# Parallel attention and gated-GELU block: which engine adds the second P-times-V bank, and in which slots a unit's scores and masks stand

## The chip, the cores and the metric

The program runs on one core of a Trainium2 chip. The metric is device time in microseconds of one execution. The core has five engines that run their own instruction queues in order: TensorE (PE in the profile; its weight loads are shown as PEld), VectorE (DVE), ScalarE (ACT), GpSimd (POOL) and SyncE (SP, which here only issues DMAs). Matmuls write into PSUM, eight banks of 128 partitions by 512 f32 columns; POOL does not touch PSUM in this kernel.

## The reference, cut to what matters

```python
x = A_x                                        # (1, 2048, 640)
xn = layernorm(x)
q, k, v = split(xn @ wqkv)                     # 32 heads of 20
scores = q @ k.T * 20 ** -0.5
mask = (i - j >= 0) & (i - j < 256)            # sliding window of 256 keys
o = softmax(where(mask, scores, -1e9)) @ v     # "P times V"
h = gelu(xn @ w_gate) * (xn @ w_up)            # 1728 wide
return x + o @ wo + h @ w_down
```

Everything is f32. The kernel reaches that precision by splitting operands into a high and a low part and adding three products.

## The kernel before, in words

**Stages.** A first stage normalises and transposes x. The second, the attention, takes about half of the span. Then come the rest of the gate and up products, and last the down projection and the output projection. The change touches the attention stage alone.

**Units.** The 32 heads are cut into 8 groups of 4, the 2048 queries into 4 chunks of 512, so there are 32 units `u`, with chunk `c = u % 4`. `attention()` (L789) runs 33 rounds of `NS = 14` slots; round `u` computes the scores of unit `u` and, in its slot 0, P times V of unit `u - 1`. The order of PE's, ACT's, DVE's and POOL's instructions in this stage is the order in which the Python code emits them (`manual_schedule`). SP is not in that list: the order of its DMAs is chosen by the framework's planner, so DMAs can be issued earlier than the slot in which the code names them.

**What a slot emits.** First the actions due in it (`tick()`; `defer(n, fn)` sets an action `n` slots later). Then, in some slots, two pairs of row maxima (`pull_max`, `max_pair`, L461): matmuls into two buffers `ps_m` out of a ring of four (`psm`), and two DVE reductions (L490), each followed by a short read of its accumulator. The maxima run ahead of the scores by two units. In slot 0 two pairs come before P times V and two behind. Then scores (`exp_piece`, L531): for score `s` of a unit, `s // 4` is the bank of keys and `s % 4` the head; PE writes `ps_e` (L545), ACT takes the exponential into P (L547). Last, `pull_fill(RATE / NS)` emits 42.2 / 14, about three, matmuls of the projection work that fills the slots (L105). Small DVE operations of that work which fall due are put in a list (`late`) and emitted by `flush()`.

**Two PSUM buffers shared.** Scores and P times V share a ring of two buffers (`psx`, tag "ex"). P times V takes both at once: `os[0]` and `os[1]`, the sums over the lower and the upper 64 key rows of each block. The next unit's score 0 takes the buffer of `os[0]`, score 1 that of `os[1]`; each waits until the buffer has been read out.

**Read-out before.** ACT copies `os[0]` to `ob` (L592) and `os[1]` to `oc`, a part of the old P (L593); three slots later POOL adds the two (`join`, L596); five slots later five DMAs store `ob` (L600, L601).

**Masks.** `pieces(c)` (L512) lists the three banks of P in the order X, Z, Y. One slot after a bank's fourth head, `clear` (L551) lets POOL zero what lies outside the window, four heads in one instruction (L558 for the diagonal, L561 for the far edge): X three instructions, Y three, Z two in chunks 1 to 3; in chunk 0, where P has no earlier keys, two, three and one. Scores stand in the odd slots 1 to 11, two a slot; in slot 1 one fill matmul is emitted between the two. So X is masked in slot 4, Z in slot 8 and Y in slot 12, and P times V (L586) starts two slots after that.

**Loads.** `load_stack` (L446) loads the q and k tiles of unit `u + 3`, six DMAs each (L455); the code names k in slot 9 and q in slot 12. The k buffer being overwritten is that of unit `u - 1`, which unit `u` still reads in X and Z.

Of the kernel before, what the change touches and what calls it, by code (L numbers as in the profile page):

```python
# [19 lines left out]
C = 512  # L20
# [11 lines left out]
RATE = 42.2  # L32
V1_SLOT = 158
MXD = 7
KSLOT = 9
LAG = 3, 5, 4, 4, 4, 4, 3, 3, 4, 3, 2, 1, 1, 1
NFA = 6
HD = D // 2
# [27 lines left out]
def block_kernel(ctx, tc, x, wqk, wv, wgu, wdo, wdl, out):  # L66
    nc = tc.nc
# [130 lines left out]
    def at(slot, fn, *a):  # L198
        acts.setdefault(slot, []).append((fn, a))
# [244 lines left out]
    ap = pr.enter_context(tc.tile_pool(name="ap", bufs=2, side="right", reuse_waits="tile"))  # L444

    def load_stack(u, which=(0, 1)):  # L446
        g, c = divmod(u, NC)
        for m in range(80 * g // 128, (80 * g + 79) // 128 + 1):
            assert all((m + 5 * i, c) in done for i in which), (u, m)

        for i in which:
            dst, src, top, again = ((qs[u % NQ], qd[c], 1, 2), (ks[u % NK], kd[c], 0, 0))[i]
            for j in (0, 2):
                for p, part, n in ((j * 32, top, 2), (j * 32 + 2 * DH, again, 1), (64 - j * 32, 0, 3)):
                    nc.sync.dma_start(dst[p:p + DH * n, j:j + 2].rearrange("p j t -> p (j t)"),  # L455
                                      src[g, part:part + n].rearrange("s (d j) t -> (s d) (j t)",
                                                                      j=4)[:, j * C:(j + 2) * C])
# [54 lines left out]
    def pieces(c):  # L512
        b = 4 * c
        X = [(b, 0, 0, 384)] + ([(b - 2, 384, 0, 128)] if c else [])
        Y = [(b + 1, 0, 128, 384), (b + 3, 384, 384, 128)]
        Z = ([(b - 1, 0, 0, 256)] if c else []) + [(b + 2, 256, 256, 256)]
        return X, Z, Y

    def diag_tail(kb, col, q0, n, c):
        r = []  # L520
# [8 lines left out]
    pts = {}  # L529

    def exp_piece(u, s):  # L531
        g, c = divmod(u, NC)
        bi, j = divmod(s, 4)
        bank = pieces(c)[bi]
        q = qs[u % NQ]
        if j == 0:
            pts[u, bi] = ap.tile([128, 4, C], F32, name="P", tag="P", bufs=3)
        pt = pts[u, bi]
        lo = min(p[1] for p in bank)
        hi = max(p[1] + p[3] for p in bank)  # L540
        ps = psx.tile([128, C], F32, name="ps_e", tag="ex")
        for kb, col, q0, n in sorted(bank, key=lambda p: p[3]):
            k = ks[(u - (kb < 4 * c)) % NK]
            kc = kb % 4 * 128
            nc.tensor.matmul(ps[:, col:col + n], k[0:QROWS, j, kc:kc + 128], q[0:QROWS, j, q0:q0 + n],  # L545
                             start=True, stop=True)
        nc.scalar.activation(pt[:, j, lo:hi], ps[:, lo:hi], AF.Exp, scale=SCALE)  # L547
        if j == 3:
            defer(1, clear, u, bi)

    def clear(u, bi):  # L551
        c = u % NC
        pt = pts[u, bi]
        for p in pieces(c)[bi]:
            for col, diag in diag_tail(*p, c):
                a = pt[:, :, col:col + 128]
                if diag:
                    nc.gpsimd.affine_select(out=a, in_=a, pattern=[[0, 4], [1, 128]], compare_op=OP.is_ge,  # L558
                                            fill=0.0, base=0, channel_multiplier=-1)
                else:  # L560
                    nc.gpsimd.affine_select(out=a, in_=a, pattern=[[0, 4], [-1, 128]], compare_op=OP.is_ge,  # L561
                                            fill=0.0, base=-1, channel_multiplier=1)

    def av_unit(u):
        g, c = divmod(u, NC)
        v = vtiles[g]
        os = [psx.tile([128, C], F32, name="ps_o", tag="ex") for _ in range(2)]
        place = {kb - 4 * c: (pts[u, bi], col, q0) for bi, bank in enumerate(pieces(c)) for kb, col, q0, n in bank}

        def half(d, r):  # L570
            i = 2 * d + r
            return d, r, max(0, 64 * i), min(C, 64 * i + 320)

        steps_ = [((0, 0), (0, 1)), ((2, 0), (-1, 1)), ((-1, 0), (2, 1)), ((1, 0), (1, 1)),
                  ((3, 0), (-2, 1)), ((-2, 0), (3, 1))]
        todo = [half(*x) for pair in steps_ for x in pair if x[0] in place]
        begun_, left = set(), [sum(t[1] == r for t in todo) for r in range(2)]
        for d, r, qa, qb in todo:
            pt, col, q0 = place[d]
            kb = 4 * c + d  # L580
            assert (id(v), kb) in done, (u, kb)
            left[r] -= 1
            rows = slice(64 * r, 64 * r + 64)
            for j in range(4):
                w0_ = kb * 84 + 21 * j
                nc.tensor.matmul(os[r][32 * j:32 * j + 32, qa:qb], v[rows, w0_:w0_ + 32],  # L586
                                 pt[rows, j, col + qa - q0:col + qb - q0], start=r not in begun_,
                                 stop=not left[r], skip_group_check=True, tile_position=(64 * r, 32 * j))
            begun_.add(r)
        ob, oc = ap.tile([128, C], F32, name="ob", tag="ob", bufs=1), pts[u, 2][:, 0]  # L590
        lo = 0 if c else 64
        nc.scalar.activation(ob, os[0], AF.Copy)  # L592
        nc.scalar.activation(oc[:, lo:], os[1][:, lo:], AF.Copy)  # L593

        def join():
            nc.gpsimd.tensor_tensor(out=ob[:, lo:], in0=ob[:, lo:], in1=oc[:, lo:], op=OP.add)  # L596
# [169 lines left out]
    NU = NG * NC  # L766
    stream = ((u, i) for u in range(NU) for i in range(8))
    fill = filler()
    debt = [0.0]

    def pull_max(n, slot):
        for _ in range(n):
            x = next(stream, None)
            if x is None:
                return
            max_pair(*x)
            if x[1] == 7:
                at(slot + (MXD if slot >= 0 else 4), max_end, x[0])

    def tick():  # L780
        todo = [y for t in sorted(t for t in acts if t <= now[0]) for y in acts.pop(t)]
        return sorted(todo, key=lambda y: y[0] is max_end)

    def pull_fill(n):
        debt[0] += n
        while debt[0] > 0:
            debt[0] -= next(fill, 1.0)

    def attention():  # L789
        now[0] = -1  # L790
        load_stack(0)
        load_stack(1)
        load_stack(2)
        for i, (p, k, half) in enumerate((p, k, half) for p in range(NC // 2) for k in range(2) for half in range(2)):
            for j, fn in enumerate(x_sums(p, k, half)):
                at(XS0 + XSN * i + 2 * j, fn)
        for i in range(12):
            now[0] = i - 13
            for fn, a in tick():
                fn(*a)  # L800
            if i % 2 == 0:
                pull_max(2, now[0])
            flush()
            pull_fill(2 * RAMP)
        pull_fill(GAP)
        for u in range(NU + 1):
            for i in range(NS):
                T = now[0] = NS * u + i
                for fn, a in tick():
                    fn(*a)  # L810
                if i in (0, 5, 9) or T == 3:
                    pull_max(2, T)
                if i == 0 and u:
# [599 lines left out]
    for n, (p, k) in enumerate(steps):  # L1413
        i = n % (NQD + 1)
# [71 lines left out]
```

## Time and profile before

| | |
|---|---|
| median of 3 runs | 1060.9 us (1057.14 to 1061.3) |
| the profiled execution's own time | 1059.57 us |
| its span | 1057.7 us |
| granted PE clock | 0.998 |
| PE busy | 1042.1 us (99%) |
| PE weight loads busy | 837.7 us (79%) |
| DVE, ACT, POOL busy | 722.2, 532.1, 376.0 us |
| first and last P times V | 106.1 and 624.9 us from the span's start |

One round of 14 slots takes about 16.8 us, a slot about 1.2 us. In the timeline a row is one or more like instructions that follow each other: its start, its length, engine, line, operation, and in brackets the idle time of that engine before it with what ended it. PE's ends are modelled: a matmul that waits can be shown as busy because the one before it is drawn long, so waits are read both from PE and from PEld rows.

### The profile page before, as it was taken

To read this page: it belongs to the slowest core of one execution; us is meant where nothing else is said; L and a number is where in the kernel's file an instruction comes from. 1 tells how busy PE (TensorE), PEld (TensorE's weight loads), DVE (VectorE), ACT (ScalarE), POOL (GpSimd) and SP (SyncE) were. 2 spreads that over 40 slices of the span, in tenths; PEclk is the share of its full clock that TensorE was granted. 3 is DMA by queue.
4 is the path that set the end of the run, shared out by engine and by line. 5 is a ranking of instruction groups with operands and counts; after the bars stand their busy time and mean duration, and the time that the engine had idled before them with its cause. 6 is when DMAs were issued, how large, how long until landed. Compare 5 with 4: busy or idle time off the path is not lost.

```text
span 1057.7 us, 25616 instructions
## 1 busy us (share of the span) xinstructions
PE 1042.1 (99%) x9429; PEld 837.7 (79%) x9429; DVE 722.2 (68%) x1985; ACT 532.1 (50%) x1120; POOL 376.0 (36%) x550
## 2 busy tenths in 40 slices
PE   8999999999999999999999999999999999999998
PEld 7977666666678766676666778888888999999998
DVE  7745656565554566766666537787775869888887
ACT  4434665566756566565665665223324544333332
POOL 6021765778664484647556451111100000000000
PEclk9999999999999999999999999999999999999999
DMA  5552353546453253434334125576667774443333
GB/s 204 186 157 71 106 175 109 149 122 191 128 159 94 77 167 102 148 100 138 106 111 128 41 82 198 185 252 235 232 234 265 257 235 128 127 138 110 122 128 105
DMA packets 105190, 158.74 MB, mean 150 GB/s; under 512 B 15420, under 2 KB 60092, under 8 KB 105064
## 3 DMA queue, kind: packets, MB, share of 16 engines
q1 hardware_dynamic: 102680, 150.95, 44.7%
q10 hardware_dynamic: 2384, 6.16, 1.8%
q8 instruction: 74, 1.21, 0.5%
q14 instruction: 52, 0.43, 0.1%
HBM read 101.78 MB, written 54.92 MB: 148 GB/s over the span
## 4 chain that ended last, share of the span: by engine, by line
PE 82%; DVE 6%; POOL 4%; issue 3%; DMA 3%; ACT 2%; SPq 1%; ACTq 0%; DVEq 0%; POOLq 0%
PE ps_d L105 24%; PE ps L1202 17%; PE ps_g L935 16%; PE ps_e L545 7%; PE ps_v L105 6%; PE ps_o L586 5%; PE ps_m L480 4%; POOL pt L247 1%; PE ps_g L105 1%; DVE junk L490 1%; DVE ss L1040 1%; POOL P L561 1%; POOL P L558 1%; DMA hr<-hd 1%; DMA stg<-wtd 1%
## 5 line engine op out<-in xcount | busy, mean ns | idle before, releaser
L490 DVE CUSTOM_DVE_ANT_0 junk<-ps_m,mask 128x320 bf16<-128x320 f32 (+2 forms) x512 | 243.1, 475 | 166.2 <-PE ps_m L480 108.4
L547 ACT ACTIVATE P<-ps_e 128x512 f32<-128x512 f32 (+2 forms) x384 | 198.7, 571 | 94.7 <-PE ps_e L545 85.4
L1202 PE MATMUL ps<-wb,at 128*128 128x320 f32 x999 | 157.1, 310 | 2.2 <-DVE at L1040 2.2
L1202 PEld LDWEIGHTS ps<-wb,at 128*128 128x128 f32 x999 | 149.6, 189 | 3.0 <-DVE at L1040 2.7
L105 PE MATMUL ps_d<-xh,wql 128*128 128x512 f32 x430 | 131.4, 415 | 0.0
L105 PE MATMUL ps_d<-xl,wqh 128*128 128x512 f32 x430 | 130.2, 412 | 0.0
L105 PE MATMUL ps_d<-xh,wqh 128*128 128x512 f32 x430 | 130.0, 413 | 0.0
L558 POOL TENSOR_SCALAR_AFFINE_SELECT P<-P 128x512 f32<-128x512 f32 x128 | 83.5, 653 | 102.7 <-ACT P L547 100.3
L545 PE MATMUL ps_e<-qs,ks 124*128 124x128 bf16 (+2 forms) x704 | 117.7, 278 | 0.7 <-ACT P L547 0.4
L105 PEld LDWEIGHTS ps_d<-xl,wqh 128*128 128x128 f32 x430 | 78.7, 189 | 15.0 <-issue 1.6
L105 PEld LDWEIGHTS ps_d<-xh,wql 128*128 128x128 f32 x430 | 78.4, 189 | 14.6 <-issue 1.2
L1202 PE MATMUL ps<-wt,at 128*128 128x320 f32 x552 | 90.0, 312 | 0.0
L105 PEld LDWEIGHTS ps_d<-xh,wqh 128*128 128x128 f32 x430 | 78.2, 189 | 14.6 <-issue 1.1
L545 PEld LDWEIGHTS <-ks 124*128 124x128 bf16 x704 | 49.6, 98 | 50.3 <-issue 36.7
L1202 PEld LDWEIGHTS ps<-wt,at 128*128 128x128 f32 x552 | 83.8, 189 | 0.2
L561 POOL TENSOR_SCALAR_AFFINE_SELECT P<-P 128x512 f32<-128x512 f32 x112 | 71.2, 646 | 27.8 <-ACT P L547 27.8
L1156 ACT ACTIVATE at<-ss 128x512 fp32r<-128x512 f32 x59 | 37.3, 632 | 86.5 <-DVE ss L1040 86.5
L586 PE MATMUL ps_o<-P,v 64*32 64x320 f32 (+4 forms) x2816 | 76.0, 348 | 1.1 <-POOL P L561 0.8
L247 POOL TENSOR_TENSOR pt<-r,pt 128x512 bf16<-128x512 f32 x40 | 46.6, 1166 | 76.8 <-ACT pt L246 75.3
L586 PEld LDWEIGHTS ps_o<-P,v 64*32 64x32 f32 x2816 | 48.5, 106 | 26.8 <-POOL P L561 3.6
L480 PE MATMUL ps_m<-ks,qs 60*64 60x320 bf16 (+3 forms) x1472 | 62.6, 260 | 3.0 <-DVE mx L490 1.2
L480 PEld LDWEIGHTS <-qs 60*64 60x64 bf16 x1472 | 28.2, 105 | 41.9 <-issue 37.2
(195 smaller groups left out, 1742.8 us busy)
## 6 DMA issues: line engine op xcount, KB each, us to landing
hr<-hd SPq DMA_DIRECT2D x104, 128.0 KB
hd<-he SPq DMA_DIRECT2D x50, 256.0 KB
wr<-wgu SPq DMA_DIRECT2D x27, 320.0 KB
qs<-qd SPq DMA_DIRECT2D x64, 120.0 KB
ks<-kd SPq DMA_DIRECT2D x64, 120.0 KB
xi<-x SPq DMA_DIRECT2D x16, 320.0 KB
qs<-qd SPq DMA_DIRECT2D x64, 80.0 KB
ks<-kd SPq DMA_DIRECT2D x64, 80.0 KB
```

Of the source, the lines that this page charges most:

```text
L105: nc.tensor.matmul(ps, a(k), b(k), start=n == 0, stop=n == 3 * nk - 1)
L247: nc.gpsimd.tensor_tensor(out=pt[:, l, :], in0=r, in1=pt[:, 1, :], op=OP.subtract)
L480: nc.tensor.matmul(ps[64 * h:64 * h + 64, col:col + w], q[rows, j, q0:q0 + 64], ks_, start=True, stop=True, tile_position=(64 * r, 64 * h))
L490: nc.vector.tensor_tensor_reduce(out=junk[:, 0:n], in0=ps[:, 320 - n:320], in1=mask[:, 320 - n:320], scale=1.0, scalar=NEG, op0=OP.add, op ...
L545: nc.tensor.matmul(ps[:, col:col + n], k[0:QROWS, j, kc:kc + 128], q[0:QROWS, j, q0:q0 + n], start=True, stop=True)
L547: nc.scalar.activation(pt[:, j, lo:hi], ps[:, lo:hi], AF.Exp, scale=SCALE)
L558: nc.gpsimd.affine_select(out=a, in_=a, pattern=[[0, 4], [1, 128]], compare_op=OP.is_ge, fill=0.0, base=0, channel_multiplier=-1)
L561: nc.gpsimd.affine_select(out=a, in_=a, pattern=[[0, 4], [-1, 128]], compare_op=OP.is_ge, fill=0.0, base=-1, channel_multiplier=1)
L586: nc.tensor.matmul(os[r][32 * j:32 * j + 32, qa:qb], v[rows, w0_:w0_ + 32], pt[rows, j, col + qa - q0:col + qb - q0], start=r not in begun ...
L935: nc.tensor.matmul(ps, i, j, start=first and n == 0, stop=n == len(work) - 1, skip_group_check=True)
L1156: nc.scalar.activation(hi[:, 3:7], s, AF.Copy)
L1202: nc.tensor.matmul(ps[bank][:, 0:HD], *work[bank][j], start=bank not in begun, stop=final[p, bank] == n and j == len(work[bank]) - 1, skip ...
```

## The change

- `join` moves from POOL to DVE: DVE adds `os[1]`, read in PSUM, to `ob` and writes `ob`. ACT's copy of `os[1]` is gone, and with it `oc`. `join` stands in slot 0 between the two pairs of maxima that follow P times V. The stores are deferred by three slots in place of five.
- The first two scores of a unit no longer share slot 1: score 0 stays, score 1 stands in slot 2 (table `EXPS`). The single fill matmul between the two is gone, and the slot's fill is emitted whole behind score 0.
- The banks are in the order X, Y, Z. Z, the bank made of two 256-wide pieces, has its masks made by pairs of heads: two heads in slot 10, two in slot 12.
- P times V takes the blocks in an order in which those of Z come last.
- q and k of unit `u + 3` are both named in slot 12.

```diff
-KSLOT = 9
+KSLOT = 12
+EXPS = {1: (0,), 2: (1,), 3: (2, 3), 5: (4, 5), 7: (6, 7), 9: (8, 9), 11: (10, 11)}
...
-        return X, Z, Y
+        return X, Y, Z
...
-        if j == 3:
-            defer(1, clear, u, bi)
-
-    def clear(u, bi):
+        if bi == 2 and j % 2:
+            defer(1, clear, u, bi, slice(j - 1, j + 1))
+        elif j == 3:
+            defer(1, clear, u, bi, slice(0, 4))
+
+    def clear(u, bi, js):
...
-                a = pt[:, :, col:col + 128]
+                a, n = pt[:, js, col:col + 128], js.stop - js.start
...
-        steps_ = [((0, 0), (0, 1)), ((2, 0), (-1, 1)), ((-1, 0), (2, 1)), ((1, 0), (1, 1)),
-                  ((3, 0), (-2, 1)), ((-2, 0), (3, 1))]
+        steps_ = [((0, 0), (0, 1)), ((1, 0), (1, 1)), ((3, 0), (-2, 1)), ((-2, 0), (3, 1)),
+                  ((2, 0), (-1, 1)), ((-1, 0), (2, 1))]
...
-        ob, oc = ap.tile([128, C], F32, name="ob", tag="ob", bufs=1), pts[u, 2][:, 0]
-        lo = 0 if c else 64
+        ob = ap.tile([128, C], F32, name="ob", tag="ob", bufs=1)
         nc.scalar.activation(ob, os[0], AF.Copy)
-        nc.scalar.activation(oc[:, lo:], os[1][:, lo:], AF.Copy)
 
         def join():
-            nc.gpsimd.tensor_tensor(out=ob[:, lo:], in0=ob[:, lo:], in1=oc[:, lo:], op=OP.add)
+            lo = 0 if c else 64
+            nc.vector.tensor_tensor(out=ob[:, lo:], in0=os[1][:, lo:], in1=ob[:, lo:], op=OP.add)
...
-        defer(3, join)
-        defer(5, store)
+        defer(3, store)
+        return join
...
                 if i == 0 and u:
-                    av_unit(u - 1)
+                    join = av_unit(u - 1)
                     flush()
-                    pull_max(2, T)
-                if i % 2 and i < 12 and u < NU:
-                    exp_piece(u, i - 1)
-                    if i == 1 and u:
-                        pull_fill(1)
-                        debt[0] -= 1
-                    exp_piece(u, i)
+                    pull_max(1, T)
+                    join()
+                    pull_max(1, T)
+                if u < NU:
+                    for s in EXPS.get(i, ()):
+                        exp_piece(u, s)
                 flush()
-                if u + 3 < NU and i in (KSLOT, 12):
-                    load_stack(u + 3, (int(i == KSLOT),))
+                if u + 3 < NU and i == KSLOT:
+                    load_stack(u + 3)
```

More of the change, by code (lines that the diff above doesn't have):

```diff
@@ L555, in clear @@
             for col, diag in diag_tail(*p, c):
-                a = pt[:, :, col:col + 128]
+                a, n = pt[:, js, col:col + 128], js.stop - js.start
                 if diag:
-                    nc.gpsimd.affine_select(out=a, in_=a, pattern=[[0, 4], [1, 128]], compare_op=OP.is_ge,
+                    nc.gpsimd.affine_select(out=a, in_=a, pattern=[[0, n], [1, 128]], compare_op=OP.is_ge,
                                             fill=0.0, base=0, channel_multiplier=-1)
                 else:
-                    nc.gpsimd.affine_select(out=a, in_=a, pattern=[[0, 4], [-1, 128]], compare_op=OP.is_ge,
+                    nc.gpsimd.affine_select(out=a, in_=a, pattern=[[0, n], [-1, 128]], compare_op=OP.is_ge,
                                             fill=0.0, base=-1, channel_multiplier=1)
```

## The prediction

> **What bounds the kernel now.** I read the page's busy table first, then its groups for the lines that the change touches, then who waited for whom, then P times V unit by unit, then the timeline of one slot 0. From the page:
>
> ```profile
> PE 1042.1 (99%) x9429; PEld 837.7 (79%) x9429; DVE 722.2 (68%) x1985; ACT 532.1 (50%) x1120; POOL 376.0 (36%) x550
> ...
> L547 ACT ACTIVATE P<-ps_e 128x512 f32<-128x512 f32 (+2 forms) x384 | 198.7, 571 | 94.7 <-PE ps_e L545 85.4
> ...
> L558 POOL TENSOR_SCALAR_AFFINE_SELECT P<-P 128x512 f32<-128x512 f32 x128 | 83.5, 653 | 102.7 <-ACT P L547 100.3
> ...
> L586 PE MATMUL ps_o<-P,v 64*32 64x320 f32 (+4 forms) x2816 | 76.0, 348 | 1.1 <-POOL P L561 0.8
> ```
>
> PE is busy for 99% of the span and bounds every stage. Work taken from POOL or ACT is therefore worth only the PE waits that it ends, and each new PE wait costs its full length. Who waited (engine, line, waited for: us in total, times, longest):
>
> ```profile
> DVE r L261 <- POOL pt L247: 12.8, 7, 2.9
> ...
> PEld ps_o L586 <- POOL P L561: 3.6, 7, 1.0
> PEld ps_o L586 <- POOL P L558: 3.4, 9, 0.4
> ...
> PE ps_m L480 <- DVE mx L490: 1.2, 4, 0.3
> ...
> PE ps_o L586 <- POOL P L561: 0.8, 2, 0.6
> ...
> PE ps_e L545 <- ACT P L547: 0.4, 1, 0.4
> ...
> PEld ps_o L586 <- ACT P L547: 0.2, 1, 0.2
> ```
>
> P times V waits for masks, some 16 times. The matmul rows show 0.8 us of it and the weight loads 7.0, for a weight load can wait while an earlier matmul still streams. The truth lies between, and the length of P times V in each unit tells it. One window for each of the 32 units, this line alone (columns: window, length, PE busy and count, weight loads; the sum is over all 32):
>
> ```profile
> 105.80:109.30 3.50, 1.93 (x64) 1.19 (x64) 1.00 0.08 27
> ...
> 140.30:143.80 3.50, 2.45 (x96) 1.71 (x96) 1.00 0.79 231
> ...
> 225.30:228.80 3.50, 2.90 (x96) 1.71 (x96) 1.00 0.71 203
> 241.90:245.40 3.50, 2.18 (x64) 0.86 (x64) 1.00 0.82 222
> ...
> sum 112.00, PE 76.00 PEld 48.47; mean PE 2.37 PEld 1.51
> ```
>
> Undisturbed it takes 1.93 us in chunk 0 and 2.45 in the others, the lengths that most windows show: 8 x 1.93 + 24 x 2.45 = 74.2. The sum is 76.0, so 1.8 us are waits inside the rows; with the 1.1 us of idle time in the page's row the waits are **2.9 us**, in seven units, five of them between 207 and 297 us where POOL has other work queued. That is what the masks cost now: 0.27%.
>
> The Trainium skill (Perfetto Trace Analysis, Identifying the Most-Contended Engine) says that matmul busy time overstates how near PE is to its limit and that the weight loads' busy share is the better measure. By it 21% of the span would be free. The trace agrees only in that the weight loads show waits which the matmul row hides; by their row alone the masks would be worth 7.0 us, by PE's alone 0.8.
>
> **The change part by part.**
>
> *Masks.* Z is masked by halves, so before P times V only two half instructions stand where three whole ones stood: 3 x 0.65 = 1.96 us become 2h. No row has a half mask; h lies between 0.33 (half of 0.653) and 0.65. Both ends take 0.66 to 1.3 us off the last stretch, and Z's blocks come last in P times V, so its masks may also end later within it. POOL's total changes by what a half costs beyond half, 0 to 1.3 us a unit, less the join's 1.25. Where the waits go, nothing else is late next: ACT's exponentials held P times V up once, for 0.2 us. I take 2.6 of the 2.9 us: **-2.6**; bounds -2.9 and 0 (should POOL's queue move the wait instead).
>
> *Join.* POOL loses 1.25 us a unit, ACT 0.58, DVE gains 0.69:
>
> ```profile
> L596 POOL TENSOR_TENSOR ob<-ob,P 128x512 f32<-128x512 f32 (+1 forms) x32 | 40.1, 1252 | 44.2 <-ACT P L593 44.2
> L593 ACT ACTIVATE P<-ps_o 128x512 f32<-128x512 f32 (+1 forms) x32 | 18.6, 581 | 0.0
> L654 DVE TENSOR_TENSOR gs<-ps_d,gs 128x512 f32<-128x512 f32 x24 | 16.5, 687 | 13.9 <-PE ps_d L105 13.9
> ```
>
> L654 has the form of the new add: PSUM and SBUF in, SBUF out. Neither POOL's nor ACT's part lies on PE's path, except where they delay others: DVE stood 12.8 us behind POOL's L247, and DVE's lateness made PE wait 1.2 us for `ps_m`. About half of that is POOL's doing: **-0.5** (0 to -1.6, with ACT's 0.4).
>
> *Score 1 behind the join.* Here a wait is added. Score 1 takes the buffer of `os[1]`, before released by ACT, now by DVE, in whose queue the join stands behind the reductions of a whole pair. Slot 0 of one round, and a place where a DVE operation without a wait follows a reduction:
>
> ```profile
> 193.28 0.08 DVE L490 DVE_READ_ACCUMULATOR2_ANT mx<- 128x1 f32 x1
> 193.28 0.69 DVE L261 TENSOR_TENSOR r<-ps_d,pt 128x512 f32<-128x512 f32 x1
> ...
> 362.61 0.47 PE L480 MATMUL ps_m<-ks,qs 60*64 60x320 bf16 x8
> 362.69 0.60 ACT L592 ACTIVATE ob<-ps_o 128x512 f32<-128x512 f32 x1 [3.94 <-PE ps_o L586]
> 362.99 0.49 DVE L490 CUSTOM_DVE_ANT_0 junk<-ps_m,mask 128x320 bf16<-128x320 f32 x1 [0.34 <-PE ps_m L480]
> ...
> 363.63 0.49 DVE L490 CUSTOM_DVE_ANT_0 junk<-ps_m,mask 128x320 bf16<-128x320 f32 x1
> ...
> 363.81 0.34 PE L545 MATMUL ps_e<-qs,ks 124*128 124x384 bf16 x1
> ...
> 363.85 0.53 PE L105 MATMUL ps_d<-xh,wqh 128*128 128x512 f32 x1
> ...
> 364.05 0.08 DVE L490 DVE_READ_ACCUMULATOR2_ANT mx<- 128x1 f32 x1
> ...
> 364.23 0.34 PE L545 MATMUL ps_e<-qs,ks 124*128 124x384 bf16 x1
> ...
> 364.27 0.49 DVE L490 CUSTOM_DVE_ANT_0 junk<-ps_m,mask 128x320 bf16<-128x320 f32 x1
> ...
> 368.24 1.32 PE L105 MATMUL ps_d<-xh,wqh 128*128 128x512 f32 x5
> ```
>
> P times V ends at 362.6; the copy of `os[0]` is done at 363.3, early enough. The first pair's second accumulator read starts at 364.05. As L261 starts with such a read, so can the join: 364.05 + 0.69 = 364.74, and PE sees a release about 0.05 us after it (396.35 + 0.08 below to 396.49). PE is ready for score 1 at 364.23 plus the two fill matmuls that now stand ahead of it besides the one already there, 2 x 0.23 (five in 1.32 us, the last drawn 0.40): 364.69. So PE waits **0.10 us**. I worked the same difference from the same rows of 30 rounds: where DVE has an operation of the fill ahead of the pair it is 0.15 to 0.26, where P times V is the short one of chunk 0 mostly 0, else 0.02 to 0.10; in all 2.4 us. Should the join start only behind the read and its semaphore, as the next reduction does (364.27), each grows by up to 0.2 and the sum becomes some 7. I take **+3.0**, near the lower end, because L261's row is the nearest; bounds 0 and +7.
>
> The Trainium skill (VectorE: DVE Perf Modes, The DRAIN you can't avoid) has a next operation start only when the one before has emptied the pipe, which would put the sum at the upper end; the row at 193.28 shows a start together with the read, so here it doesn't hold.
>
> The pair behind the join is delayed by 0.69 us on DVE. Its buffers are next wanted in slot 5, five slots or 6 us later, against four reductions of 0.64 (362.99 to 363.63) and the join, 3.3 us of DVE work: 0. But where DVE was already late, PE waits for the pair's own buffers as now:
>
> ```profile
> 396.35 0.08 DVE L490 DVE_READ_ACCUMULATOR2_ANT mx<- 128x1 f32 x1
> 396.49 0.33 PE L480 MATMUL ps_m<-ks,qs 60*64 60x320 bf16 x3 [0.35 <-DVE mx L490]
> ```
>
> These buffers are freed by reductions that stand ahead of the join, so it adds nothing there.
>
> *Slots and order.* The number of fill matmuls and of changes between scores and fill is the same. P times V has the same matmuls; its last block is 192 columns wide and not 64, so its end can shift by 128/512 of 0.23 us, 0.06 a unit: 0, bounds -1.9 and +1.9. Score 1's exponential comes a slot later, but score 3, which takes its buffer, follows score 1 by a slot, 1.2 us, against 0.57 for the exponential: 0.
>
> *Loads and stores.* k can no longer be loaded before Z's scores in slots 9 and 11, so twelve DMAs now stand in SP's queue where six stood. Once the trace shows nearly that already, and once the tightest place for q:
>
> ```profile
> 355.96 1.03 SPq L455 DMA_DIRECT2D qs<-qd  x3
> ...
> 357.87 2.16 SPq L455 DMA_DIRECT2D qs<-qd  x3
> 360.08 1.83 SPq L455 DMA_DIRECT2D ks<-kd  x5
> ...
> 367.37 0.47 PE L480 MATMUL ps_m<-ks,qs 60*64 60x256 bf16 x16
> ...
> 141.18 2.57 SPq L455 DMA_DIRECT2D qs<-qd  x6
> ...
> 148.01 0.47 PE L480 MATMUL ps_m<-ks,qs 60*64 60x256 bf16 x16
> ```
>
> q's first use is in the maxima at 367.37. Six k DMAs behind q's last end near 362, which leaves 5 us for them to land. At 143.75 the room is 4.3 us, 2.1 after six more at 0.37 each, and stores queue there too. The trace gives no landing times. I take **+0.5**, bounds 0 and +8. The stores leave SP two slots earlier in the code; they wait for a join that now ends sooner: 0.
>
> **Sum**: -2.6 - 0.5 + 3.0 + 0.5 = +0.4 us. The profiled execution took 1059.57 us for a span of 1057.7, so 1060.0; the median of the three runs, 1060.9, is 1.3 above that execution. Half a percent, 5.3 us, is about what a measurement of this kernel can tell from no change.
>
> **The rivals.**
>
> *Slower: score 1 waits for DVE in every round.* For it: the margin is negative in most rounds already by my own sum, and a wait of 0.3 us would need no more than the join's start 0.2 later. Against: L261's row. At 0.3 us in 31 rounds less 3.1 gained: +6, about 1066. It decides from 0.27 us a round on (5.3 + 3.1 over 31). The Trainium skill (Perfetto Trace Analysis, Optimization Strategy) reads the same gap repeating on the busiest engine as too few buffers for the next tile; here they are two, and no run yet shows that gap.
>
> *Faster: masks are worth what the weight loads' row says.* 7.0 + 1.2 + 0.4 and no wait for score 1: 1051. Against: the windows add up to 2.9, and the margin.
>
> *Slower: k lands late.* Needed at slot 5. For it: 2.1 us of room at 143.75; against: most rounds leave 4 to 5. One microsecond late in eight rounds gives +8, 1068; it decides from 5.5 us in all.
>
> *The masks aren't cheaper.* A half that costs a whole (h = 0.65) puts 2.6 us a unit where 1.3 stood, which gives POOL's saving back, and exponentials of the other two heads might wait for the first two's masks. Then the 2.6 aren't gained: +3.0, 1063, still within half a percent.
>
> **How the numbers follow.** Forecast 0.58 (1056 to 1065), masks no cheaper 0.09, faster 0.09, score 1 slower 0.16, k late 0.08. Faster by over 0.5%: the fast rival and 0.01 of the forecast's own edge, 0.10. Slower: 0.14 of score 1, 0.05 of k late and 0.03 of the forecast's edge, 0.22. Within: the rest, 0.68. The range leaves out the fast rival and the upper part of the slow ones: 1055 to 1068.
>
> **What would show it.** P times V at 1.93 and 2.45 us in nearly every window (else the masks' step is wrong); `ps_e` of score 1 started some 0.05 us behind the join's end, with a longer gap in front than score 0 has (its mean is the step's price); PE waits for `ps_m` no more frequent; L480 in slot 5 without a DMA as releaser. The prediction is wrong if that gap is above 0.27 us, or if the planner orders SP so that q or k arrives behind its first use.

## The result, and the profile after

The changed kernel takes 1064.64 us (median of 20 runs, 1061.02 to 1067.52) against 1059.95 us (20 runs, 1056.27 to 1063.85) for the kernel before: ratio **1.0046, 95% interval [1.0034, 1.0057]**. The forecast of 1060.0 us was 4.6 us low. The time lies inside the range, but the forecast's "no change" is wrong: the kernel is slower by 0.46%.

The profiled execution took 1061.55 us, 3.1 below the median of its runs, so two executions can't simply be subtracted. The view of busy time by windows, cut at the first and the last P times V, shows why. Its columns are the window, its length, and busy time with counts for PE, PEld, DVE, ACT and POOL. Before:

```profile
106.10:624.80 518.70, 515.19 (x6178) 358.88 (x6174) 310.11 (x1104) 320.42 (x684) 320.35 (x483) 1.00 0.41 122
624.80:1057.70 432.90, 427.33 (x2529) 393.46 (x2528) 344.15 (x670) 164.90 (x296) 23.22 (x17) 1.00 0.55 183
```

After:

```profile
106.10:629.20 523.10, 518.90 (x6186) 359.88 (x6174) 321.20 (x1135) 307.69 (x653) 289.58 (x507) 1.00 0.39 121
629.20:1059.70 430.50, 425.78 (x2529) 391.98 (x2528) 342.73 (x671) 164.08 (x295) 20.47 (x14) 1.00 0.55 184
```

The stretch from the first P times V to the last, "the stretch" from here on, is longer by **4.3 us** by the starts of the two (106.12 to 624.87 before, 106.18 to 629.25 after). That is 0.41% of the time, near the measured ratio. What follows it is code that the change doesn't touch; it was 2.4 us shorter in this execution. So the loss is in the attention stage, and the stretch is the measure for what follows; each kernel's stretch is that of one profiled execution.

From the page after:

```profile
PE 1044.7 (99%) x9429; PEld 837.7 (79%) x9429; DVE 731.8 (69%) x2017; ACT 518.7 (49%) x1088; POOL 343.0 (32%) x574
...
L561 POOL TENSOR_SCALAR_AFFINE_SELECT P<-P 128x512 f32<-128x512 f32 (+1 forms) x160 | 88.7, 555 | 165.5 <-ACT P L548 162.7
...
L589 PE MATMUL ps_o<-P,v 64*32 64x320 f32 (+4 forms) x2816 | 78.3, 349 | 1.8 <-ACT P L548 1.0
```

POOL lost 33 us of work and ACT 13, DVE gained 10, and the kernel is slower: neither POOL nor ACT was the bound. P times V, from which 2.6 us were to go, grew from 76.0 to 78.3 us in PE's row, and its idle time from 1.1 to 1.8. The waits after (engine, line, waited for: us in total, times, longest):

```profile
PEld L546 <- DVE ob L598: 7.1, 22, 0.5
...
PEld ps_o L589 <- POOL P L561: 2.1, 3, 1.1
...
PE ps_o L589 <- ACT P L548: 1.0, 1, 1.0
PE ps_e L546 <- ACT P L548: 0.8, 3, 0.4
PE ps_o L589 <- POOL P L561: 0.6, 1, 0.6
```

Of the sixteen waits for masks that the weight loads showed, three are left, of 0.7 us on average where they were of 0.4 (7.0 / 16). A new wait is now the longest of those for another engine in the attention stage's PE and PEld rows: scores behind the join (`ob`, L598). The windows of P times V, one for each unit (columns as in the prediction, without the weight loads), show both that and something else:

```profile
105.88:109.88 4.00, 1.94 (x64) 1.00 0.06 19
122.84:126.84 4.00, 3.11 (x96) 1.00 0.64 195
...
157.66:161.66 4.00, 2.55 (x96) 1.00 0.49 159
...
226.66:230.66 4.00, 2.88 (x96) 1.00 0.65 206
...
377.97:381.97 4.00, 2.54 (x64) 1.00 0.46 136
...
sum 128.00, PE 78.30; mean PE 2.45
```

In chunks 1 to 3 an undisturbed P times V now takes **2.55 us where it took 2.45**; 22 of the 24 windows read so. That is 24 x 0.10 = 2.4 us, with the same matmuls. The waits inside the rows are 78.3 less 8 x 1.94 and 24 x 2.55: 1.6 us, where they were 1.8.

The starts of the matmuls tell the two apart without the modelled ends. From its first matmul to the next one of another line, an undisturbed P times V of chunks 1 to 3 takes 2.376 us before and 2.483 after (1.860 and 1.873 in chunk 0). What a unit takes beyond that is waits: 2.84 us in sum before, in seven units (1, 6, 7, 8, 10, 11, 16), and 2.26 us after, in three (0.7 us at unit 1, 0.3 at 7, 1.2 at 16). So the waits inside P times V fell by 0.6 us, and its length took more than that back.

The new length sits at its end. The last matmul of unit 3's P times V and the matmul behind it, before, where P times V starts at 157.49:

```profile
159.72 0.22 PE L586 MATMUL ps_o<-P,v 64*32 64x64 f32 x1
159.87 0.33 PE L480 MATMUL ps_m<-ks,qs 60*64 60x320 bf16 x4
```

And after, where it starts at 157.96:

```profile
160.19 0.32 PE L589 MATMUL ps_o<-P,v 64*32 64x192 f32 x1
160.45 0.33 PE L481 MATMUL ps_m<-ks,qs 60*64 60x320 bf16 x4
```

The last of the 96 starts 2.23 us behind the first in both. The next line starts 0.146 us behind it where the last block is 64 columns wide and 0.253 us where it is 192 wide.

Added up from the starts of the PE rows in each of the 31 rounds of the stretch, before to after: P times V +2.0 us (2.6 of new length less 0.6 of waits); from its end to score 0, -1.0; score 0 to score 2, +2.25; score 2 to the next P times V, +1.1. Together +4.3. The second is a gain, 0.8 us of it at unit 17, where PE had waited for DVE (the prediction's row at 396.49). The first, third and fourth each need a cause.

### The profile page after: what moved, and what is told of

It is laid out like the page before. It is cut to its first block, busy times and chain, and to the rows that moved or that the text cites. A ratio compares the mean times of both kernels' runs of the same rounds, so it can differ in the third digit from the quotient of the medians.

```text
span 1059.7 us, 25662 instructions
## 1 busy us (share of the span) xinstructions
PE 1044.7 (99%) x9429; PEld 837.7 (79%) x9429; DVE 731.8 (69%) x2017; ACT 518.7 (49%) x1088; POOL 343.0 (32%) x574
## 4 chain that ended last, share of the span: by engine, by line
PE 88%; DVE 5%; POOL 2%; ACT 2%; issue 1%; DMA 1%; DVEq 0%; SPq 0%; ACTq 0%; POOLq 0%
PE ps_d L106 26%; PE ps L1203 19%; PE ps_g L936 16%; PE ps_e L546 8%; PE ps_v L106 6%; PE ps_o L589 6%; PE ps_m L481 4%; DVE junk L491 1%; PE ps_g L106 1%; DVE ss L1041 1%; DMA stg<-wtd 1%; POOL pt L248 1%; ACT P L548 1%; PE ps_t L184 0%; DVE at L1041 0%
## 5 line engine op out<-in xcount | busy, mean ns | idle before, releaser
L548 ACT ACTIVATE P<-ps_e 128x512 f32<-128x512 f32 (+2 forms) x384 | 201.6, 570 | 112.2 <-PE ps_e L546 105.1
L561 POOL TENSOR_SCALAR_AFFINE_SELECT P<-P 128x512 f32<-128x512 f32 (+1 forms) x160 | 88.7, 555 | 165.5 <-ACT P L548 162.7
L564 POOL TENSOR_SCALAR_AFFINE_SELECT P<-P 128x512 f32<-128x512 f32 (+1 forms) x136 | 76.1, 568 | 14.0 <-ACT P L548 12.5
L589 PE MATMUL ps_o<-P,v 64*32 64x320 f32 (+4 forms) x2816 | 78.3, 349 | 1.8 <-ACT P L548 1.0
```

The lines of the kernel that those rows point to most:

```text
L561: nc.gpsimd.affine_select(out=a, in_=a, pattern=[[0, n], [1, 128]], compare_op=OP.is_ge, fill=0.0, base=0, channel_multiplier=-1)
L564: nc.gpsimd.affine_select(out=a, in_=a, pattern=[[0, n], [-1, 128]], compare_op=OP.is_ge, fill=0.0, base=-1, channel_multiplier=1)
```

## The experiments

Each kernel was timed in five rounds beside the kernel before. "Stretch" is the difference of its profiled stretch to that of before (518.75 us).

| kernel | ratio to before, 95% | stretch, us |
|---|---|---|
| the change | 1.0046 [1.0034, 1.0057] | +4.3 |
| e1 change, narrow block pairs last | 1.0044 [1.0027, 1.0061] | +4.2 |
| e2 change, join ahead of both pairs | 1.0035 [1.0022, 1.0049] | +3.75 |
| e3 both of these | 1.0015 [1.0004, 1.0026] | +2.2 |
| e4 change, score 1 in slot 1 | 1.0223 [1.0202, 1.0244] | +23.1 |
| e5 before, join's part alone (join first) | 1.0012 [0.9999, 1.0025] | +1.2 |
| e6 before, banks' part alone | 1.0015 [1.0000, 1.0030] | +1.3 |
| e7 e3 with whole masks | 1.0037 [1.0019, 1.0055] | +3.3 |
| e8 before, k loaded in slot 12 | 1.0003 [0.9987, 1.0018] | +0.3 |
| e9 e3, masks put in at once | 1.0024 [1.0012, 1.0037] | +2.4 |
| e10 e6, masks put in at once | 0.9987 [0.9975, 1.0000] | +0.6 |
| e11 e5, masks put in at once | 1.0048 [1.0029, 1.0066] | +5.2 |
| e12 before, masks put in at once | 1.0043 [1.0029, 1.0057] | +5.4 |
| e13 before, score 1 in slot 2 | 1.0023 [1.0008, 1.0038] | +2.0 |
| e14 e6, second half mask at once | 1.0007 [0.9990, 1.0024] | +0.9 |

The stretch divided by 1059.5 gives the measured ratio within 0.0008 for every kernel but e10 (0.0018 off). So the places found in the stretch carry the times, and waits of a few tenths of a microsecond can be followed one by one. But 0.0008 is 0.8 us: two kernels whose stretches differ by less are told apart by these places alone, not by their times.

### e1, e2, e3: the order of P times V, and the join's place

e1 changes the order of the block pairs, e2 the place of the join, e3 both:

```diff
-        steps_ = [((0, 0), (0, 1)), ((1, 0), (1, 1)), ((3, 0), (-2, 1)), ((-2, 0), (3, 1)),
-                  ((2, 0), (-1, 1)), ((-1, 0), (2, 1))]
+        steps_ = [((0, 0), (0, 1)), ((1, 0), (1, 1)), ((2, 0), (-1, 1)), ((-1, 0), (2, 1)),
+                  ((3, 0), (-2, 1)), ((-2, 0), (3, 1))]
...
-                    pull_max(1, T)
-                    join()
-                    pull_max(1, T)
+                    join()
+                    pull_max(2, T)
```

> The changed kernel with one edit: in P times V the two narrow block pairs (128 and 64 columns) come last again, behind Z's. Theory A (narrow blocks in the middle use up the weight loads' lead, so that the wide blocks behind them start at the pace of weight loads): P times V of chunks 1 to 3 goes from 2.48 back to 2.38 us from first to last start, the run is 2.4 us (0.22%) faster than the changed kernel, ratio to the kernel before 1.002. Theory B (the 0.10 us come from something else, such as masks or the end of the last block): P times V stays at 2.48, no change of time.

> The changed kernel with one edit: the join stands ahead of both pairs of maxima in slot 0. Theory A (score 1 waits for a join that stands behind a pair's reductions): the join ends near 1.4 us behind P times V in place of 2.1, the longer gap in front of score 1 goes, 2.2 us (0.2%) faster than the changed kernel, ratio to before 1.0025. Rival: reductions that start 1 us later make PE wait for its ps_m buffers in slot 5 and take the gain back; then PE's waits for DVE at the maxima grow by 1 us or more and the time is unchanged.

> The changed kernel with both edits: narrow blocks last and the join first. If the loss is made of these two (2.5 and 2.25 us), they add: 4.6 us faster than the changed kernel, ratio to before 1.000 (0.999 to 1.001). If they hide each other, or the loss lies elsewhere (k's later load, masks), the ratio stays at 1.002 or more.

P times V by windows in e1, the same units 1, 3 and 16:

```profile
122.81:126.81 4.00, 3.04 (x96) 1.00 0.68 192
...
158.27:162.27 4.00, 2.45 (x96) 1.00 0.51 147
...
378.39:382.39 4.00, 2.54 (x64) 1.00 0.57 160
...
sum 128.00, PE 76.08; mean PE 2.38
```

The 0.10 us a unit is the order's: with the narrow pairs last it is gone. Yet e1's time stayed. P times V became shorter by 0.107 us in each of the 23 units of chunks 1 to 3 in the stretch, 2.5 us, but its waits grew from 2.26 to 3.30 us, at units 1, 2 and 16: Z's blocks are read earlier, and their masks are waited for. Of the 1.55 us that P times V gained in sum, 1.4 came back: 0.67 us ahead of score 0, 0.3 between scores 0 and 1, where PE now came earlier to the same release by the join, 0.36 behind score 2. With the join put first, the same edit (e2 to e3) gained 1.5 us in the stretch, and 1.0035 became 1.0015. A gain is kept only where the next wait isn't already standing behind it.

The join, in the round of unit 15's P times V, after the change:

```profile
364.38 0.47 PE L481 MATMUL ps_m<-ks,qs 60*64 60x320 bf16 x8
...
365.62 1.00 PE L106 MATMUL ps_d<-xh,wqh 128*128 128x512 f32 x3
...
365.81 0.08 DVE L491 DVE_READ_ACCUMULATOR2_ANT mx<- 128x1 f32 x1
365.81 0.69 DVE L598 TENSOR_TENSOR ob<-ps_o,ob 128x512 f32<-128x512 f32 x1
...
366.56 0.32 PE L546 MATMUL ps_e<-qs,ks 124*128 124x384 bf16 x1
```

P times V ends at 364.4. The join starts 1.43 us later, together with the second accumulator read, lasts 0.69, and score 1 starts 0.06 behind its end: the step that the prediction described. The Trainium skill (VectorE: DVE Perf Modes, The DRAIN you can't avoid) has the next operation start only when the pipe is empty, but adds that one which is not held starts earlier; this row, like the prediction's at 193.28, shows a start together with the read. In e2 the same join starts 0.67 us after P times V's end, as soon as ACT's copy of `os[0]` is done, and score 1 waits no more:

```profile
365.20 0.47 PE L481 MATMUL ps_m<-ks,qs 60*64 60x320 bf16 x8
...
365.87 0.69 DVE L598 TENSOR_TENSOR ob<-ps_o,ob 128x512 f32<-128x512 f32 x1 [0.75 <-ACT ob L594]
...
366.44 1.00 PE L106 MATMUL ps_d<-xh,wqh 128*128 128x512 f32 x3
367.28 0.34 PE L546 MATMUL ps_e<-qs,ks 124*128 124x384 bf16 x1
```

From the fill's first matmul to score 1 it is 0.84 us here (366.44 to 367.28) and 0.94 in the changed kernel (365.62 to 366.56): a wait of 0.10 us in this round, as forecast. Score 0 to score 1 falls from 30.34 to 28.35 us over 31 rounds. So score 1's wait was **2.0 us** in sum, against 3.0 forecast. Of these, the stretch of e2 kept only 0.56: 0.6 came back ahead of score 0, most of it at unit 17, 0.3 between scores 1 and 2, and 0.6 behind score 2; the ratio came to 1.0035, where 1.0025 was expected. e3 came to 1.0015 where 1.000 was expected; what is left is the matter of e5, e6 and e13.

### e4: how much the slot between score 0 and score 1 hides

```diff
-EXPS = {1: (0,), 2: (1,), 3: (2, 3), ...
+EXPS = {1: (0, 1), 3: (2, 3), ...
```

> The changed kernel with one edit: score 1 stands in slot 1 directly behind score 0, as many fill matmuls as before behind it. If score 1 waits for the join's end near 2.17 us behind P times V: it is now ready at 1.2 + 0.24 = 1.44, so PE waits about 0.7 us a round instead of 0.07, +20 us on the changed kernel, ratio to before 1.023. If the release comes otherwise (the buffer of score 1 freed earlier), the time stays within 2 us of the changed kernel.

The waits in e4:

```profile
PE ps_e L546 <- DVE ob L598: 12.8, 24, 0.8
...
PEld L546 <- DVE ob L598: 19.0, 23, 1.1
```

The loss is 1.0223, as expected from the theory that score 1 waits for the join. The slot that the change puts between the two scores is needed: without it the stretch is another 18.8 us longer. Against the kernel before, score 0 to score 2 takes 21.6 us more in e4, so the weight loads' row (19.0) is nearer to the whole wait than PE's (12.8). It is no price for every wait, though: in the changed kernel the same row said 7.1 us for the wait of score 1, which was 2.0.

### e5, e6, e8, e13: the two halves of the change, each alone

e5 has the join on DVE ahead of both pairs, the scores in slots 1 and 2 and the earlier store, with the banks, masks, order and loads of before; e6 the banks X, Y, Z, the half masks, both loads in slot 12 and the narrow pairs last, with the join and the scores of before; e8 only the loads; e13 only the scores' slots.

e5, its core:

```diff
-        defer(3, join)
-        defer(5, store)
+        defer(3, store)
+        return join
...
+                    join()
                     pull_max(2, T)
...
+                    for s in EXPS.get(i, ()):
+                        exp_piece(u, s)
```

e6, its core:

```diff
-        return X, Z, Y
+        return X, Y, Z
...
+        if bi == 2 and j % 2:
+            defer(1, clear, u, bi, slice(j - 1, j + 1))
...
-KSLOT = 9
+KSLOT = 12
```

e8, its core:

```diff
-KSLOT = 9
+KSLOT = 12
```

e13, its core:

```diff
-                    exp_piece(u, i - 1)
-                    if i == 1 and u:
-                        pull_fill(1)
-                        debt[0] -= 1
-                    exp_piece(u, i)
+                    for s in EXPS.get(i, ()):
+                        exp_piece(u, s)
```

> The kernel before with the join's part alone: the add on DVE, put ahead of both pairs, a unit's scores in slots 1 and 2 as in the changed kernel, the store at slot 3; banks, masks, the order of P times V and the loads as before. The version with this join and the new banks and masks stood at 1.0015. Theory A (what is left of the loss sits in the banks and their loads; the join, put first, costs nothing and takes 1.25 us a unit off POOL's queue, so that about half of the 2.9 us of mask waits go): 1058.4 us against 1059.9, ratio 0.9985; P times V about 1.5 us shorter in sum than before. Theory B (the join on DVE delays the pairs and the scores behind it): 1061.3, ratio 1.0015, with score 0 to score 2 longer by over 0.5 us in sum and the wait from score 2 to the next P times V longer by about 1.5.

> The kernel before with the other part alone: banks X, Y, Z, Z's masks by head pairs, both loads in slot 12, P times V with the narrow block pairs last; the join on POOL and the scores as before. Theory A (the banks and loads carry the rest of the loss): 1062.2 us, ratio 1.0022, the time from score 2 to the next P times V longer by 1 to 1.5 us in sum, and mask waits no smaller than before (2.5 to 4 us), since POOL still has its join. Theory B (the join carries it, and the cheaper masks gain): 1058.5, ratio 0.9987, P times V shorter by 1.5 us in sum.

> The kernel before with one number changed: k is loaded in slot 12 with q, and not in slot 9. If the loads standing together delay the stores of kd and qd, and with them ACT (the 1.05 us lost at unit 7): 1061.0, ratio 1.0010, ACT waits for stores of pt 5 us in sum where there were 3.0. If that loss comes from the banks or the planner's timing: 1060.0, ratio 1.0000, ACT's waits as before.

> The kernel before with one thing changed: score 1 in slot 2 and not in slot 1 (the fill matmul between scores 0 and 1 goes too, as in the change); join, banks, masks and loads as before. If score 1's slot is the price of the join's part (its exponential comes later, and score 2 or 3 waits for it where ACT is late): the four waits of a score for ACT at units 2, 7, 16 and 27 appear, 0.5 us between scores 0 and 2 too, 1060.9 beside 1059.8, ratio 1.0010. If the add on DVE is: 1059.8, ratio 1.0000, those places as before.

**The join's part** (e5: join, slots and store) took 1.0012: no gain where 0.9985 was expected. P times V was as long as before (72.25 against 72.35 us in the stretch), so taking 1.25 us a unit from POOL ended hardly any of the mask waits. The loss is 0.5 us between scores 0 and 2, and 0.9 behind score 2. **e13** puts that on the slots, not on the join: score 1 moved alone costs 2.0 us in the stretch (1.0023 in time, where 1.0010 was expected), 0.5 in the first place and 1.6 in the second, all of these 1.6 in the four rounds that the expectation named. Adding the join on DVE to that (e13 to e5) gains 0.8, which the two ratios alone wouldn't tell apart. The waits for ACT in e13's stretch, 1.4 us where before had 0.4:

```profile
PE ps_e L546 <- ACT P L548: 1.4, 4, 0.4
```

One of them in the changed kernel, in the round of unit 2's P times V, PE above, ACT below:

```profile
145.24 0.39 PE L546 MATMUL ps_e<-qs,ks 124*128 124x128 bf16 x2
...
146.18 0.39 PE L546 MATMUL ps_e<-qs,ks 124*128 124x128 bf16 x2
146.81 0.38 PE L546 MATMUL ps_e<-qs,ks 124*128 124x128 bf16 x2 [0.24 <-ACT P L548]
...
144.70 0.60 ACT L548 ACTIVATE P<-ps_e 128x512 f32<-128x512 f32 x1 [0.99 <-PE ps_e L546]
145.19 0.59 ACT L642 ACTIVATE gs<-ps_d 128x512 f32<-128x512 f32 x1
145.67 0.61 ACT L643 ACTIVATE he<-ps_d 128x512 f32<-128x512 f32 x1
146.14 1.68 ACT L548 ACTIVATE P<-ps_e 128x512 f32<-128x512 f32 x3
```

The same place before:

```profile
144.65 1.09 ACT L547 ACTIVATE P<-ps_e 128x512 f32<-128x512 f32 x2 [0.48 <-PE ps_e L545]
145.62 0.61 ACT L640 ACTIVATE gs<-ps_d 128x512 f32<-128x512 f32 x1
146.10 0.62 ACT L641 ACTIVATE he<-ps_d 128x512 f32<-128x512 f32 x1
```

Before, score 1's exponential stood beside score 0's, ahead of the fill's two ACT operations. In slot 2 it stands behind them, 1.0 us later, and score 3, which takes score 1's buffer, waits.

**The banks alone** took 1.0015. P times V is 0.6 us longer than before in the stretch: the waits at units 6, 8, 10 and 11 shrink by 1.6 us, those at units 1, 2 and 16 grow by 2.2. **The loads alone** (e8) took 1.0003, 0.3 us in the stretch, which its interval can't tell from nothing: the forecast's +0.5 was not too small. e6 lost 0.9 us at unit 6's round, which e8 does not show (0.14). There ACT stood behind a store of `pt` for 2.05 us in the changed kernel where it had stood 1.12, its exponentials came late, and P times V of unit 7 waited 1.0 us for ACT, the new `ps_o` wait above. Why that store landed later is open; SP issued other loads ahead of it in the two kernels.

### e7: what the half masks are worth

```diff
-        if bi == 2 and j % 2:
-            defer(1, clear, u, bi, slice(j - 1, j + 1))
-        elif j == 3:
+        if j == 3:
             defer(1, clear, u, bi, slice(0, 4))
```

> The changed kernel with the narrow block pairs last and the join first (ratio 1.0015 in its run), and Z's masks whole again, two instructions behind score 11 instead of four in two steps. If the split is worth what the prediction gave it (P times V waits for two halves instead of two wholes, 0.5 us a unit less): P times V waits in nearly every unit, 31 x 0.3 to 0.5 us longer, 1071 to 1077, ratio 1.011 to 1.016. If the waits come from other work that stands ahead in POOL's queue, as the idle times of units 1, 7 and 16 suggest: no more than 1 us, 1062, ratio 1.002.

P times V became 1.5 us longer than in e3, at units 6, 7, 9, 10 and 11, and the time 1.0037. Neither number came out. The halves do help where POOL has nothing else to do in between, by 0.2 to 0.5 us in five units, and not in all 31: in most units two whole masks (1.3 us) are done in time too. At units 1, 2 and 16 the whole masks are better, by 0.45 us in sum; the next runs show why.

### e9 to e12, e14: masks ahead of the fill work

At unit 16, after the change, POOL does this while P times V, begun at 378.27, runs to 381.38:

```profile
378.50 0.46 POOL L629 TENSOR_TENSOR wql<-wr,wqh 128x128 fp32r<-128x128 f32 x1
378.91 0.40 POOL L561 TENSOR_SCALAR_AFFINE_SELECT P<-P 128x256 f32<-128x256 f32 x1
379.29 0.45 POOL L629 TENSOR_TENSOR wql<-wr,wqh 128x128 fp32r<-128x128 f32 x1
379.70 0.72 POOL L726 TENSOR_TENSOR tx<-tx,xl 128x256 f32<-128x256 f32 x1
380.38 0.40 POOL L561 TENSOR_SCALAR_AFFINE_SELECT P<-P 128x256 f32<-128x256 f32 x1
```

A half costs 0.40 us, so it is cheaper than a whole, as forecast (bounds 0.33 and 0.65). But the second half starts 1.47 us behind the first: fill work that falls due in between, 0.45 + 0.72 us, now stands between the halves. In e9 to e12 the last bank's masks are emitted directly behind their exponentials, ahead of that slot's fill; in e14 the second half only.

e9 (on e3) and e10 (on e6):

```diff
-            defer(1, clear, u, bi, slice(j - 1, j + 1))
+            clear(u, bi, slice(j - 1, j + 1))
```

e11 (on e5) and e12 (on the kernel before):

```diff
-            defer(1, clear, u, bi)
+            clear(u, bi) if bi == 2 else defer(1, clear, u, bi)
```

e14 (on e6):

```diff
-            defer(1, clear, u, bi, slice(j - 1, j + 1))
+            clear(u, bi, slice(2, 4)) if j == 3 else defer(1, clear, u, bi, slice(0, 2))
```

> The version with both edits (narrow block pairs last, join first; 1.0015 in its run), with one thing more: Z's half masks are put into POOL's queue right behind the exponentials of their head pair, ahead of the fill work of that slot, and not at the start of the next slot. If the waits of P times V come from fill work that stands ahead of the masks in POOL's queue (at units 1 and 16, about 1 us each): P times V falls from 72.8 us in sum to about 70.4, and the ratio to 0.9992 (1058.6 us beside 1059.5). If POOL, now waiting for the exponentials, holds the fill's own POOL work back and DVE and PE behind it: P times V still shorter, but the time between longer by as much, ratio 1.0015 or more.

> The new banks, halves and loads alone, with the join left on POOL (1.0015 in its run), and the half masks put into the queue at once. If the queue's order makes the waits: P times V from 73.0 to about 70.5 us in sum, ratio 0.9992. If POOL's waiting only moves them: 1.0015. Against the version with both edits it tells what the join on DVE is worth once the masks are out of the way: the same if the join's part is worth nothing, 0.001 lower if the 0.5 us in the scores and the 0.9 us behind them are the join's price.

> The join's part alone, put first (1.0012 in its run), with the old banks, and the last bank's whole masks put into POOL's queue at once behind its scores. If the queue's order makes the waits: P times V from 72.25 to about 70.8 us in sum, ratio 0.9998. If three whole masks behind the last exponential are too long whatever stands ahead of them: P times V 71.5 or more, ratio 1.0005 to 1.0012.

> The kernel before, with only the last bank's whole masks put into POOL's queue at once. If the waits come from the queue's order: P times V from 72.35 to about 70.8 us in sum, 1057.9 us beside 1059.5, ratio 0.9985: the gain that was expected of the change, without the change. If the masks' own length makes them: ratio 0.9995 to 1.0000, P times V 71.8 or more.

> The new banks, halves and loads, the join on POOL, and only the second half mask of Z put into POOL's queue at once (both at once took 0.9987). If the 1.5 us lost ahead of score 0 at units 9 and 10 come from all the masks ahead of POOL's L247: half of it stays, P times V at 70.6 us in sum as there, ratio 0.9980. If the first half's place decides nothing: as there, 0.9987. If P times V waits again at units 1 and 16: 1.000.

With half masks at once (e9, e10, e14) most waits inside P times V are gone. Unit 1 and the sum in e10:

```profile
124.22:128.22 4.00, 2.45 (x96) 1.00 0.65 195
...
sum 128.00, PE 75.08; mean PE 2.35
```

The waits left inside the rows are 75.08 - 74.2 = 0.8 us. By the starts, e6 had 3.45 us of waits and e10 has 1.05. So the queue's order made the wait at unit 1 (1.1 us, gone) and about half of that at unit 16 (1.4 us, now 0.7). In e9, against e3, 2.2 us went from P times V, and 2.4 us appeared elsewhere: the ratio is 1.0024, the rival's outcome. With whole masks (e11, e12) the kernels are slower than without: 1.0048 and 1.0043, where 0.9985 to 1.0012 was expected. At unit 9 in e12, POOL, DVE and PE:

```profile
258.53 0.64 POOL L558 TENSOR_SCALAR_AFFINE_SELECT P<-P 128x512 f32<-128x512 f32 x1 [1.06 <-ACT P L547]
...
261.00 1.16 POOL L247 TENSOR_TENSOR pt<-r,pt 128x512 bf16<-128x512 f32 x1
...
262.20 0.69 DVE L261 TENSOR_TENSOR r<-ps_d,pt 128x512 f32<-128x512 f32 x1 [4.23 <-POOL pt L247]
...
263.35 0.29 PE L480 MATMUL ps_m<-ks,qs 60*64 60x320 bf16 x1 [0.72 <-DVE mx L490]
```

POOL idles 1.06 us for the exponential, its three masks push L247 back, DVE's L261 waits for L247 and holds the reductions of the maxima, and PE waits for their buffers, 3.3 us in all between 240 and 290 us. What P times V waited for is paid one queue further on. e14 shows it too: the loss ahead of score 0 at units 9 and 10 stays at 1.5 us with one half at once, so it doesn't come from the first half's place.

e10 reads 0.9987, the lowest ratio of all, and beats the changed kernel by far. That it beats the kernel before is not shown: its interval ends at 1.0000, its own stretch is 0.6 us longer than that of before, and e14, with the same waits in P times V, came to 1.0007. Against e9, which differs by the join's part, e10's stretch is 1.9 us shorter, 0.5 of it between scores 0 and 2 and 1.15 behind score 2: the places of e13 again.

## Why the prediction was wrong, point by point

**Masks, -2.6: wrong.** The price of a half was right (0.40 us), the mechanism was not: the sum looked at how many mask instructions stand last and not at what else POOL's queue holds between them. In the changed kernel the waits inside P times V fell by 0.6 us, from 2.84 to 2.26; with the banks alone (e6) they rose to 3.45. That Z's masks may end later because its blocks come last was right: with the narrow pairs last (e1) the waits were 1.0 us longer. "Should POOL's queue move the wait instead" was the bound of 0, and it happened: the waits at units 6, 8, 10 and 11 went, those at units 1 and 16 grew.

**Slots and order, 0: wrong**, by two terms, and this is the larger error of the sum. The prediction saw that the last block would be 192 columns wide and not 64, priced these 128 columns by a fill matmul's row at 0.06 us, and then put the term at nothing. They cost 0.107 us (0.253 less 0.146) in each of 24 units, some 2.5 us, more than the bound of 1.9; undone, 1.5 us of it came back with the join first, and 0.1 without. And "score 3 follows score 1 by a slot, 1.2 us, against 0.57 for the exponential" left out ACT's queue, where the fill's two operations, 1.0 us, now stand ahead of that exponential: e13 prices the slots at 2.0 us.

**Join, -0.5: right in sign, for another reason in part.** On top of the slots the join gained 0.8 us (e13 to e5), not by mask waits, which hardly changed (2.83 to 2.74 us), but mostly in one place: 0.9 us at unit 1's round, where the one wait of a score for ACT that the kernel before had (0.4 us in its row) is gone; the prediction had these 0.4 us only in its bound. The gain in `ps_m` waits that the term counted on doesn't show: from P times V to score 0, e5 is 0.1 us shorter than the kernel before, and e13 as much.

**Score 1 behind the join, +3.0: right in mechanism**; it measured 2.0, inside the bounds of 0 and 7.

**Loads and stores, +0.5: about right in size** (e8: +0.3, for the loads). The late store at unit 6 came with the banks, not with the loads.

**The rivals.** "Score 1 waits in every round" at 0.3 us did not happen: the wait was 2.0 / 31 = 0.06 us on average. k did not land late: no matmul row of the changed kernel waits for a load of k. "The masks aren't cheaper" named the right term, though by a dearer half and not by the queue. No rival held the order of the blocks or ACT's queue, by e2 to e3 and e13 worth 1.5 and 2.0 us, beside score 1's 2.0. Term by term the runs give -0.6 for the masks, -0.8 for the join, +2.0 for score 1, +2.5 for the order, +2.0 for the slots and +0.3 for the loads: +5.4 where +0.4 was forecast and +4.3 measured. The parts cover for each other, so they don't simply add up.

**Which row tells the masks' worth.** The forecast's reading between the two rows, 2.9 us, was right: by the starts it is 2.84. In e10 and e9 the queue's order took away 2.4 and 2.2 us of the 3.45 and 3.25 that e6 and e3 had. The Trainium skill (Perfetto Trace Analysis, Identifying the Most-Contended Engine) calls matmul busy time no good measure of how near PE is to its limit, and names the weight loads' busy share as one of two better ones. The Trainium skill doesn't say there that matmul time overstates, as the prediction has it, and it prices no single wait. Here the row is no price either: it said 7.0 for the masks' 2.84, 7.1 for score 1's 2.0, and 19.0 for e4's 21.6.

## What to carry to other kernels

Before a step is moved to another slot, write down the queue of each in-order engine at its new place, with the operations of the fill that will then stand ahead of it: two of the three steps that failed here, the halves on POOL and the exponential on ACT, were cheap instructions that got behind other work. Where the order of the same matmuls changes, price the last one by its own width and by rows of its own kind, and don't put the term at zero. Expect that a wait which is taken from one queue may be handed to the next one, as in e9, e11 and e12. With stages this regular, comparing the starts of a few marked instructions round by round finds losses of 0.1 us which totals of busy time hide.

## What was unexpected in the hardware

The same 96 matmuls of P times V take 2.45 us with the two narrowest block pairs last (before and e1) and 2.55 us with them ahead of the 256- and 192-wide pairs, in every undisturbed unit of chunks 1 to 3. The last matmul starts 2.23 us behind the first in both orders; the difference lies behind it, 0.146 us to the next line where it is 64 columns wide and 0.253 where it is 192. Why the last start stays in its place was not separated. An add on DVE that reads PSUM starts together with the accumulator read of the reduction before it (365.81), and PE starts on the released buffer 0.06 us after its end.
